# Causal attention into a channel mix on one core: another order on every engine, and a sixth of the operations on another engine

## The chip, the cores and the metric

The kernel runs on one core of a Trainium2 chip. TensorE (PE) multiplies matrices into PSUM, VectorE (DVE), ScalarE (ACT) and GpSimd (POOL) do the elementwise work, SyncE (SP) issues the DMAs. The metric is the device time of one execution in microseconds, the median of three runs.

## The reference

Attention first: four batches of twelve heads, 448 tokens, head dimension 64. Its output, with the heads side by side as 768 features, goes into a channel mix with a hidden width of 1024.

```
scores = q @ k.T / 8;  future tokens masked;  attn = softmax(scores);  x = attn @ v
x_prev = x shifted down by one token, first row 0
xk = mu_k*x + (1-mu_k)*x_prev;   xr = mu_r*x + (1-mu_r)*x_prev
k  = relu(xk @ w_k);   v = (k*k) @ w_v;   r = sigmoid(xr @ w_r)
out = r * v
```

## The kernel before

Two heads make a *pair*; there are 24 pairs, six to a batch, each giving one tile xt of 128 features by 448 tokens. The score rows of a pair are split into chunks of 112 tokens. For each pair TensorE makes the scores (L405, L418), VectorE takes the row maxima (L435), ScalarE or VectorE scales them (L447, L449), ScalarE takes the exponentials (L458). In batch 0 TensorE then transposes the exponentials (L663) and a copy brings them to SBUF (L674); later the probabilities are split into two f16 parts (L639, L643) and transposed by DMA. The product with v (L705) and an evacuation (L722) give xt; the inverse row sums reach xt by way of two small matmuls and a copy (L616, L620, L626, L636).

Once a pair's xt is there, two weighted copies are mixed: a scaling (L249 on ScalarE, L251 on VectorE, L255 on GpSimd, all through the helper `scaled`) and a multiply-add on VectorE (L749), and in later batches a split into f16 parts (L756, L760). A batch's projections run over its six pairs: mk (1024 wide, from xk and w_k) and mr (768 wide, from xr and w_r). In batch 0 they are fp32 matmuls (L981), in later batches three f16 matmuls to a step (L966). k is clipped and squared (L989 or L991, L1005 or L1007), scaled by a common factor that is brought through TensorE (`across`, L270 and L281) and split into f16 parts: the high part by `scaled`, the low part by one instruction on VectorE (L1053) or two on GpSimd (L255 and L1056). Its product with w_v is mv; the last multiplication (L1076) reads mv and r, which was copied out of PSUM (L1061). The accumulators share few PSUM banks, so a new one waits for the instruction that empties an older one.

The weights come in by DMA through three staging buffers: the raw words are taken apart (L840, L848 or L850, L854), the largest element of each half row is found (`w_half`, L806, whose main output `junk` is thrown away), scales are made (L814 to L822) and the f16 parts written (L249, L251 or L255, and L884 or L887). Loads of q and k of a pair have three buffers.

What sets the order: every operation is recorded in a `Plan` (L39) and issued by `Plan.run` in the order of a number each, from the row `starts` in `CHOICE`. Some 722 operations can go to more than one engine, and a letter each in `engines` (A, D, P) says to which. `fills` says where idle matmuls stand (`idle`, L298): pieces of two matmuls of 64 columns, whose results nobody reads. An engine runs its instructions in the order of issue and waits for whatever an instruction needs.

## Time and profile before

| | us |
|---|---|
| median of three runs | 484.56 (483.99 to 485.06) |
| the profiled execution | 485.16 |
| its span in the trace | 483.2 |
| busy in the span: TensorE, VectorE, ScalarE, GpSimd | 466.2, 371.5, 290.3, 202.9 |

The span runs from the first instruction to the last; 1.96 us of the profiled execution lie outside it. A busy share is a mean over stages that differ: the first 60 us are attention of batch 0 with the weights' preparation beside it, later stages are mostly matrix products. TensorE's busy time holds the fillers too.

### The profile page before, as it was taken

The page shows a single profiled execution, that of the slowest core. Times are in us where ns is not written, and L with a number is a line of the kernel's source. Part 1 is how long each engine was busy: PE and PEld are TensorE (multiplying, and loading weights), DVE is VectorE, ACT ScalarE, POOL GpSimd, SP SyncE. Part 2 cuts the span into 40 slices and gives each one's busy share as a digit, 9 for nine tenths or more (in the row PEclk, how much of TensorE's full clock was granted, in tenths as well). Part 3 has the DMA queues.
Part 4 walks back from the last instruction along what each step waited for, and adds up shares of the span by engine and source line. Part 5 has one row for each costly group of instructions (what it writes and reads, how often), then busy time and mean ns, then how long its engine had stood idle before and what let it go on. Part 6 is the DMA issues. An engine that isn't in the chain of part 4 may idle for free.

```text
span 483.2 us, 9633 instructions
## 1 busy us (share of the span) xinstructions
PE 466.2 (96%) x3685; PEld 271.3 (56%) x3685; DVE 371.5 (77%) x724; ACT 290.3 (60%) x814; POOL 202.9 (42%) x174
## 2 busy tenths in 40 slices
PE   8898899999999899999999899999999999999996
PEld 6566665455546566655555556655566565555553
DVE  5999899998898899998788998834879986337021
ACT  5999998996526976678959632645647710110500
POOL 4341461216732263747735723671557665003000
PEclk9999999999999999999999999999999999999999
DMA  8997466881107689391158587353155771000011
GB/s 319 298 333 255 152 213 208 201 217 39 39 1 155 139 191 199 109 165 38 40 102 167 142 177 131 89 112 78 39 96 98 169 146 39 0 1 0 1 57 58
DMA packets 94846, 60.60 MB, mean 125 GB/s; under 512 B 83408, under 2 KB 86480, under 8 KB 94032
## 3 DMA queue, kind: packets, MB, share of 16 engines
q1 hardware_dynamic: 94800, 59.98, 49.7%
q8 instruction: 29, 0.48, 0.4%
q14 instruction: 17, 0.14, 0.1%
HBM read 33.82 MB, written 5.51 MB: 81 GB/s over the span
## 4 chain that ended last, share of the span: by engine, by line
PE 70%; DVE 10%; ACT 9%; DMA 7%; issue 2%; POOL 1%; DVEq 0%; POOLq 0%; ACTq 0%; SPq 0%
PE mk L966 17%; PE mv L966 17%; PE mr L966 9%; PE s L418 7%; PE mk L981 6%; PE bank L705 5%; DMA pT<-p 5%; PE mr L981 4%; ACT e L458 4%; PE s L405 2%; DVE s L435 2%; DMA wraw<-in_w_r_dram 1%; ACT junk L806 1%; DVE pT L674 1%; ACT wk L840 1%
## 5 line engine op out<-in xcount | busy, mean ns | idle before, releaser
L966 PE MATMUL mv<-k,wv 128*128 128x448 f16 x576 | 113.8, 353 | 1.7 <-DVE a L1076 1.7
L458 ACT ACTIVATE e<-s,st 112x224 f32<-112x224 f32 (+3 forms) x192 | 93.3, 497 | 10.2 <-DVE st L449 4.5
L966 PE MATMUL mk<-xk,wk 128*128 128x448 f16 x432 | 83.6, 353 | 0.0
L966 PEld LDWEIGHTS <-wv 128*128 128x128 f16 x576 | 54.5, 98 | 50.9 <-issue 2.5
L435 DVE TENSOR_REDUCE s<-s 112x2 f32<-112x224 f32 (+3 forms) x96 | 70.2, 742 | 13.0 <-PE s L418 11.8
L966 PEld LDWEIGHTS <-wk 128*128 128x128 f16 x486 | 46.5, 98 | 44.6 <-issue 2.2
L966 PE MATMUL mr<-xr,wr 128*128 128x448 f16 x270 | 56.3, 353 | 0.0
L643 DVE TENSOR_TENSOR p<-e,p 112x1120 f16<-112x1120 f32 x27 | 37.4, 1389 | 7.1 <-ACT p L639 3.7
L1076 DVE SCALAR_TENSOR_TENSOR a<-mv,kap,a 128x448 f32<-128x448 f32 x24 | 16.1, 674 | 34.7 <-PE mv L966 34.6
L458 ACT ACTIVATION_READ_ACCUMULATOR e<-s,st 112x1 f32 x192 | 40.1, 209 | 0.0
L981 PE MATMUL mk<-xk,wk 128*128 128x448 f32 x96 | 38.2, 546 | 0.3 <-DVE xk L749 0.3
L966 PEld LDWEIGHTS <-wr 128*128 128x128 f16 x270 | 25.4, 98 | 22.4 <-issue 0.3
L1061 ACT COPY a<-mr 128x448 f32<-128x448 f32 x16 | 8.5, 534 | 37.9 <-PE mr L966 17.7
L749 DVE SCALAR_TENSOR_TENSOR xf<-xt,shares,xf 128x448 f32<-128x448 f32 x36 | 29.8, 841 | 1.0 <-POOL xf L255 0.8
L705 PEld LDWEIGHTS <-vs 112*64 112x64 f16 x648 | 26.9, 110 | 6.1 <-issue 5.1
L705 PE MATMUL bank<-pT,vs 112*64 112x224 f16 (+1 forms) x648 | 29.7, 245 | 0.5 <-DMA pT<-p 0.5
L981 PE MATMUL mr<-xr,wr 128*128 128x448 f32 x72 | 29.2, 547 | 0.0
L850 POOL TENSOR_SCALAR wraw<-wraw 128x768 int32<-128x768 uint16 (+1 forms) x13 | 16.3, 1257 | 25.8 <-DVE pT L674 10.7
L981 PEld LDWEIGHTS mk<-xk,wk 128*128 128x128 f32 x96 | 17.5, 190 | 16.3 <-issue 15.4
L369 POOL TENSOR_TENSOR ql<-qk,qh 128x896 fp32r<-128x896 f32 x8 | 21.0, 2630 | 12.6 <-issue 7.3
L418 PE MATMUL s<-ql,qh 64*112 64x112 f32 (+3 forms) x144 | 25.7, 352 | 0.4 <-POOL ql L369 0.4
L989 ACT ACTIVATE a<-mk 128x448 f32<-128x448 f32 x24 | 13.1, 547 | 21.1 <-PE mk L966 20.5
(219 smaller groups left out, 909.5 us busy)
## 6 DMA issues: line engine op xcount, KB each, us to landing
qk<-in_qk_dram SPq DMA_DIRECT2D x24, 448.0 KB, 3.7
wraw<-in_w_k_dram SPq DMA_DIRECT2D x6, 1024.0 KB, 10.3
wraw<-in_w_v_dram SPq DMA_DIRECT2D x8, 768.0 KB, 4.6
vraw<-in_v_dram SPq DMA_DIRECT2D x24, 224.0 KB, 3.0
out_dram<-a SPq DMA_DIRECT2D x24, 224.0 KB, 2.1
wraw<-in_w_r_dram SPq DMA_DIRECT2D x6, 768.0 KB, 4.7
pT<-p SPq DMA_TRANSPOSE x36, 4.9
muT<-in_mu_dram SPq DMA_DIRECT2D x1, 6.0 KB, 13.2
```

Source lines behind the costliest of these rows:

```text
L369: tt[e](t, qkt.pop(w), qkh[w].bitcast(F32), ALU.subtract)
L418: nc.tensor.matmul(s[:CP, j, o : o + n], q_[rows, 0, c * CP : (c + 1) * CP], k_[rows, 1, :n], start=False, stop=c == max(STEPS[g]) and i = ...
L435: nc.vector.tensor_reduce(stat[w][:, c, :] if flipped(w) else most(w, g, c, c + 1), s[:CP, :, o : o + CP * (c + 1)], AX.X, ALU.max, negate ...
L458: nc.scalar.activation(em[w, j][:, blocks(c)].rearrange("p a b -> p (a b)"), sps[w, g][:CP, j, o : o + CP * (c + 1)], AF.Exp, bias=stat[w] ...
L643: tt[e](p[:, NB:, :CP], em.pop((w, j)), p[:, :NB, :CP], ALU.subtract)
L705: nc.tensor.matmul(px[w][64 * j : 64 * j + 64, cols], value(j, vi), p(j, pi), start=n == 0 and i == 0, stop=last and i == len(steps) - 1, ...
L749: nc.vector.scalar_tensor_tensor(f, x_of(w)[:, :S], share(w, mu, 1), f, ALU.mult, ALU.add)
L850: nc.gpsimd.tensor_scalar(t, u, TOP3, -0.499, ALU.mult, ALU.add)
L966: nc.tensor.matmul(ps, w[:, wi, cols], x[:, xi, t0 : t0 + n], start=(i == 0 and a == 0), stop=(i == steps - 1 and a == 2),)
L981: nc.tensor.matmul(mps[m, kind, o][:, :n], z[:, o * P : (o + 1) * P], x, start=i == 0, stop=i == NO - 1)
L989: nc.scalar.activation(a, mps[m, "k", f][:, :n], AF.Relu)
L1076: nc.vector.scalar_tensor_tensor(s, mps.pop((m, "v", o))[:, : M[m][2]], kap[m][:, 3:4], s, ALU.mult, ALU.mult)
```

## The change

Only three rows of `CHOICE` differ: the numbers in `starts` (2161 of them), 353 of the 722 letters of `engines` (of A, D and P there were 260, 322 and 140, now 253, 318 and 151), and `fills` (24 entries as before, but 103 pieces in place of 153, so 206 filler matmuls in place of 306, of which 20 now stand behind the start of the dense part). The list of operations is the same; a few operations take two instructions on one engine and one on another.

```
-    "fills": [[1300,14],[6745,15],[11149,16],[15068,5],[19523,3],[23646,1],...
+    "fills": [[4358,14],[9432,10],[12788,10],[16261,1],[20040,2],[25465,6],...
```

Three places, as the instructions stand on their engine. Names carry a pair's number (e_2_1 is the second head's exponentials of pair 2) or a batch and block (k2_3_5); the last number only tells tiles apart.

ScalarE at the exponentials of pair 2, up to its last one, before:

```order
L458 ACTIVATE e_2_1_491,su_2_490<-s_2_0_429,st_2_465 112x112
L806 ACTIVATE junk_91,wn_149<-wk_144 128x512
L674 COPY pT_1_0_474<-eT_1_0_2_498 112x448
L674 COPY pT_1_1_527<-eT_1_1_0_505 112x336
L447 ACTIVATE st_2_465<-s_2_1_483 112x2
L806 ACTIVATE junk_91,wn_149<-wk_144 128x512
L458 ACTIVATE e_2_0_496,su_2_490<-s_2_1_483,st_2_465 112x336
L458 ACTIVATE e_2_1_491,su_2_490<-s_2_1_483,st_2_465 112x336
L447 ACTIVATE st_2_465<-s_2_2_515 112x2
L674 COPY pT_1_1_527<-eT_1_1_2_545 112x448
L458 ACTIVATE e_2_0_496,su_2_490<-s_2_2_515,st_2_465 112x448
L458 ACTIVATE e_2_1_491,su_2_490<-s_2_2_515,st_2_465 112x448
```

and now, from the second exponential of pair 2 to the first of pair 3:

```order
L458 ACTIVATE e_2_1_405,su_2_398<-s_2_0_385,st_2_394 112x224
L458 ACTIVATE e_2_0_399,su_2_398<-s_2_0_385,st_2_394 112x112
L458 ACTIVATE e_2_1_405,su_2_398<-s_2_0_385,st_2_394 112x112
L458 ACTIVATE e_2_0_399,su_2_398<-s_2_1_415,st_2_394 112x336
L458 ACTIVATE e_2_1_405,su_2_398<-s_2_1_415,st_2_394 112x336
L840 ACTIVATE wk_144<-wraw_3_351 128x1024
L806 ACTIVATE junk_91,wn_149<-wk_144 128x512
L636 COPY xt0_92<-sp_0_462 128x448
L458 ACTIVATE e_2_1_405,su_2_398<-s_2_2_443,st_2_394 112x448
L458 ACTIVATE e_2_0_399,su_2_398<-s_2_2_443,st_2_394 112x448
L674 COPY pT_1_1_469<-eT_1_1_1_501 112x336
L458 ACTIVATE e_3_0_520,su_3_519<-s_3_0_473,st_3_515 112x112
```

Of the half-row pieces (L806) fewer stand among the exponentials: 21 stood ahead of pair 5's last one, now 10 do. Copies of L636 have come here from VectorE.

VectorE ahead of the mix of pair 5's xk (`xk_5`), before:

```order
L369 TENSOR_TENSOR ql_7_1347<-qk_7_1196,qh_7_1341 128x896
L822 RECIPROCAL wm_146<-wm_146 128x1
L722 TENSOR_TENSOR xt1_93<-bank_142,xt1_93 128x448
L435 TENSOR_REDUCE s_6_2_1316<-s_6_2_1316 112x2
L884 SCALAR_TENSOR_TENSOR wv_1138<-wz_13_1265,wm_146,wv_1138 128x768
L251 TENSOR_SCALAR xk_5_1384<-xt1_93,sharesp_154 128x448
L854 SCALAR_TENSOR_TENSOR wz_14_1349<-wz_14_1349,wraw_14_1290 128x768
L749 SCALAR_TENSOR_TENSOR xk_5_1384<-xt1_93,sharesp_154,xk_5_1384 128x448
```

and now:

```order
L722 TENSOR_TENSOR xt1_93<-bank_142,xt1_93 128x448
L435 TENSOR_REDUCE s_7_0_1190<-s_7_0_1190 112x2 x2
L449 TENSOR_SCALAR st_7_1225<-s_7_0_1190 112x4
L816 TENSOR_SCALAR wm_146<-wm_146 128x1
L884 SCALAR_TENSOR_TENSOR wv_969<-wz_12_1063,wm_146,wv_969 128x768
L818 TENSOR_SCALAR wm_146<-wm_146 128x1
L749 SCALAR_TENSOR_TENSOR xk_4_1207<-xt0_92,sharesp_154,xk_4_1207 128x448
L822 RECIPROCAL wm_146<-wm_146 128x1
L749 SCALAR_TENSOR_TENSOR xk_5_1212<-xt1_93,sharesp_154,xk_5_1212 128x448
```

The evacuation (L722) and the mix stand 20 and 17 rows earlier in the list; the last L369, L854 and L251 ahead of the mix are behind it or on other engines, and a reduction for pair 7 stands ahead of it.

GpSimd's last rows, batch 3, before:

```order
L756 CAST xk_23_5384<-xf0_23_5366 128x448
L760 TENSOR_TENSOR xk_23_5384<-xf0_23_5366,xk_23_5384 128x448
L760 TENSOR_TENSOR xr_21_5399<-xf1_21_5379,xr_21_5399 128x448
L255 TENSOR_TENSOR xf1_22_5415<-xt2_94,shares_152 128x448
L255 TENSOR_TENSOR a_156<-a_156,tf_3_5617 128x448
L1056 TENSOR_TENSOR k2_3_5_5669<-a_156,k2_3_5_5669 128x448
```

and now:

```order
L760 TENSOR_TENSOR xr_20_5300<-xf1_20_5294,xr_20_5300 128x448
L255 TENSOR_TENSOR xf1_21_5303<-xt1_93,shares_152 128x448
L760 TENSOR_TENSOR xr_21_5325<-xf1_21_5303,xr_21_5325 128x448
L255 TENSOR_TENSOR xf1_22_5328<-xt2_94,shares_152 128x448
L255 TENSOR_TENSOR a_156<-a_156,tf_3_5519 128x448
L1056 TENSOR_TENSOR k2_3_1_5526<-a_156,k2_3_1_5526 128x448
```

There k2_3_5 is block 5 of k in batch 3. Before, GpSimd made the low part of one block; now of six: behind the pair shown for block 1, five more such pairs follow, for blocks 4, 3, 6, 7 and 5.

SyncE's loads stand in another order too: qk of pair 5 behind the third load of w_r.

## Rows read from the trace of the kernel before

**Rows 1.** The profile page, parts 1 and 2: busy us (share) xinstructions; granted clock

```profile
PE 466.2 (96%) x3685; PEld 271.3 (56%) x3685; DVE 371.5 (77%) x724; ACT 290.3 (60%) x814; POOL 202.9 (42%) x174
...
PEclk9999999999999999999999999999999999999999
```

**Rows 2.** Busy us by stretch (x instructions), then PEclk, DMA share, GB/s

```profile
0.00:60.00 60.00, 52.24 (x669) 36.87 (x669) 52.13 (x113) 52.22 (x165) 22.12 (x37) 1.00 0.82 273
60.00:82.40 22.40, 21.63 (x182) 13.19 (x180) 21.46 (x42) 21.66 (x66) 9.67 (x9) 1.00 0.61 214
82.40:165.20 82.80, 81.78 (x414) 43.53 (x415) 73.64 (x164) 58.31 (x156) 31.68 (x23) 1.00 0.49 115
...
380.00:483.20 103.20, 99.55 (x618) 53.26 (x615) 44.66 (x90) 16.51 (x35) 22.80 (x18) 1.00 0.21 49
```

**Rows 3.** Fillers, by line: busy us, mean ns, then idle before

```profile
L298 PE MATMUL bank<-busy 128*128 128x64 f16 x306 | 14.3, 202 | 0.2 <-DVE xt L722 0.2
```

**Rows 4.** TensorE's timeline at 82 and at 166 us: start, length, idle before, releaser

```profile
82.43 2.52 PE L981 MATMUL mk<-xk,wk 128*128 128x448 f32 x6 [0.28 <-DVE xk L749]
...
165.96 0.73 PE L966 MATMUL mv<-k,wv 128*128 128x448 f16 x3 [1.69 <-DVE a L1076]
```

**Rows 5.** VectorE's timeline ahead of 82.43

```profile
80.84 1.53 DVE L749 SCALAR_TENSOR_TENSOR xk<-xt,sharesp,xk 128x448 f32<-128x448 f32 x1
```

**Rows 6.** Busy us between 20 and 40 us

```profile
20.00:40.00 20.00, 18.06 (x247) 13.02 (x246) 18.91 (x40) 19.97 (x67) 6.63 (x8) 1.00 0.95 320
```

**Rows 7.** VectorE's timeline at 39 us

```profile
39.48 0.67 DVE L325 TENSOR_REDUCE vm<-vraw 112x1 f32<-112x512 f32 x1
40.07 1.21 DVE L854 SCALAR_TENSOR_TENSOR wk<-wk,wraw 128x1024 uint32<-128x1024 uint32 x1
```

**Rows 8.** Single lines: count, ns min/median/max, first and last start us, form

```profile
L636 DVE COPY xt<-sp x12: 604/614/626, 19.2 to 391.7; 128x448 f32<-128x448 f32 x12
...
L636 ACT COPY xt<-sp x12: 510/534/621, 52.9 to 394.5; 128x448 f32<-128x448 f32 x12
...
L251 DVE TENSOR_SCALAR xk<-xt,sharesp x4: 443/679/1093, 35.9 to 79.6; 128x448 f32<-128x448 f32 x4
...
L369 DVE TENSOR_TENSOR ql<-qk,qh x10: 1074/1080/1275, 75.9 to 303.0; 128x896 fp32r<-128x896 f32 x10
...
L884 DVE SCALAR_TENSOR_TENSOR wv<-wz,wm,wv x6: 966/1004/1007, 74.3 to 105.2; 128x768 f16<-128x768 f32 x6
...
L854 DVE SCALAR_TENSOR_TENSOR wz<-wz,wraw x8: 942/949/959, 68.6 to 109.8; 128x768 uint32<-128x768 uint32 x8
...
L848 ACT ACTIVATE wraw<-wraw x7: 884/912/981, 47.1 to 108.4; 128x768 int32<-128x768 uint16 x7
```

**Rows 9.** ScalarE's timeline at 16 and at 59 us

```profile
16.11 0.66 ACT L806 ACTIVATE junk<-wk 128x512 f16<-128x512 f32 x1
...
16.73 0.56 ACT L458 ACTIVATE e<-s,st 112x336 f32<-112x336 f32 x1
...
59.12 0.46 ACT L458 ACTIVATE e<-s,st 112x224 f32<-112x224 f32 x1
```

**Rows 10.** The page's part 6: loads, KB each, median us from issue to landing

```profile
qk<-in_qk_dram SPq DMA_DIRECT2D x24, 448.0 KB, 3.7
```

**Rows 11.** K's scaling on GpSimd, copy of r on ScalarE, by line

```profile
L255 POOL TENSOR_TENSOR a<-a,tf x4: 932/2036/3156, 135.2 to 441.5; 128x448 f32<-128x448 f32 x4
...
L1061 ACT COPY a<-mr x16: 520/532/568, 130.8 to 453.0; 128x448 f32<-128x448 f32 x16
```

**Rows 12.** GpSimd's timeline at 249 and at 441 us

```profile
249.09 0.93 POOL L255 TENSOR_TENSOR a<-a,tf 128x448 f32<-128x448 f32 x1
...
441.49 3.16 POOL L255 TENSOR_TENSOR a<-a,tf 128x448 f32<-128x448 f32 x1 [34.23 <-DVE k L251]
444.73 1.03 POOL L1056 TENSOR_TENSOR k<-a,k 128x448 f16<-128x448 f32 x1
```

**Rows 13.** VectorE's timeline at 442 us

```profile
441.99 1.87 DVE L1053 SCALAR_TENSOR_TENSOR k<-a,tf,k 128x448 f16<-128x448 f32 x3
```

More of the change, by code (lines that the diff above doesn't have):

```diff
@@ L95 @@
-    "engines": "PPPPPPADADADAPADDDDDDDPPAAADDDDDDAADADADADPPADDDDAADDDDDADDADAADDDPDDDPPADDDAADDDPPDDADDDADDPAAPPPAPDDPDDPADPADADDADDADDAAPADPAAAAAAAAAAAADDAAADADADADPDADPDAPPPDDPDPDPDADADDDPDADDDADDAAADDPPDDADADPPADPDPDAPAPPDPDADDDAADPDDAADAAADDPDAAPDADADDDAPPDAADADAPDAPDADDADDDDDDDAAADADDAPDDDPDPAPPAPAAADDADDAPDPDAAPAADADAADADAPAAAPAPAPPDAPDDPPADDDADPADAADAAADDAAAAAAADAAAADADADADADAPADADAAAAAAAAADAAADDDAPDAADPDDDAAADADDAPDADAPDAAADADAADDDDPDPDAPPDDDDADAPAAADADDAPPAPAPDAAAPAPADADADPDPAADPDADDADDPADPDPDDPPDPDDDDDDDDDDDPDDPAPAADDADADAAADAAAADDADADPDADADADDPADDADDADDDDAADAADADADAPDAPDDAPAPADDAPDDPDADPDDPDAPPPPAPPAPPDPADAAPADADADPDAPDDPDAPADADDAPAAAPDPPDDPDPDPAADPDPPDDADAPAAPPADPPDDAADDDDDPPDDDDDDDADADADAADDDDDDDDDDDDDDDPDDDDADAAAA",
@@ new lines @@
+    "engines": "PPPPPPDAADDAPPDADDADDDPPDDDPPAADDDDADPDDADAPDADDDAADPDDDAPDADAAADAADDDPPADADDDAAAPPDADDDADDAPPPPPAPDAPPDDADDADDPDDPADADDPPDAADADAAADADDAAAAAAAAPADADADADADPDDDPDADDDPDADPDPDADPDDDPDADADAAAAADDDDDPDAPDDADDDDDADPPDDAAAAAAPPDADPPDADADPPDDPDADADDDADDDDAAADPPDDPDPDDADAAPDDADAADAPDAAPADDPPAADAPAAAADDDADDDADDDPDDPPDDADADADDAPDPPDPPPAPPDAPAAADADDDDDAPAAAAADAADAAAAADDADAPAPAPADADDDDDADAAAAAAAAADADAAAPDAADDDPDAAADADDADDPPADAADPDPDDDDDDDAPDAAPADAAADDPPAAADDDDDDDDDADAADPDADDAPDDPAAPDDPADADDADPPDAPPAPAPPADPDDDDADADAPDDDAAPDAADDDAAAADAADDDPDDDADADPPAPADADAADDDAAAAAADPPDDDDDDADDDPPDAAPPDDPPADDAPDADPPPDADPPPPDPPDDDPDAAAADPPAADDADPPPPDPAPDDDPDADDDPDADAAPPDPDDAADADDPADPDAPAPPPDDDDDPAAADADDADADDDAAAAADDDDAADADADDAPADAPAPAPAPDPDADADA",
@@ L97 @@
+    "fills": [[4358,14],[9432,10],[12788,10],[16261,1],[20040,2],[25465,6],[29602,3],[32890,1],[32891,7],[33260,1],[34435,1],[34620,3],[34945,2],[39897,3],[43831,15],[44886,2],[45393,1],[46161,3],[54848,6],[61621,2],[125763,2],[134158,4],[179277,1],[180230,3]],
 }
```

3 lines of the change are left out of this document (1 added, 2 removed).

## The prediction

> **What bounds the kernel now.** I read the page's first two parts first: TensorE is busy 96% of the span and its granted clock stands in the top digit in every slice [rows 1]. So time can only come out of TensorE's idle time, out of its filler matmuls, or out of its real work, and the real work is the same before and after. Next I read the busy times by stretch [rows 2]. TensorE is idle 7.8 us of the first 60 (60 - 52.24), 0.8 of the next 22.4, 1.0 of the 82.8 after that, 3.7 of the last 103.2. The 306 fillers take 14.3 us, all before 63.4 us [rows 3]. So some 23 us without useful work (7.8 + 0.8 + 14.3) lie ahead of 82.4 us, and far less lies behind. What ends that start is seen in TensorE's own timeline and VectorE's: the first matmul of the batch-0 projection that reads the mixed tile of pair 5 starts at 82.43, released by VectorE's mix (L749), which began at 80.84 and lasted 1.53 [rows 4, 5]. From there TensorE runs nearly without a gap; the only long one is 1.69 us at 165.96, ahead of mv_0_2, whose accumulator waits for VectorE's multiplication (L1076) [rows 4]. In the first 60 us both VectorE (52.13) and ScalarE (52.22) are full, between 20 and 40 us ScalarE 19.97 of 20 and VectorE 18.91 [rows 2, 6]. So the start is bound by the list of things that these two engines do ahead of pair 5's mix, and it gets shorter by what is taken out of that list.
>
> **The change part by part.**
> *VectorE's list up to the mix of xk_5.* An instruction there costs its duration less about 0.08 us, because the next starts before its end: the reduction at 39.48 lasts 0.67 but the next starts at 40.07, 0.59 later [rows 7]. Four copies of L636 go to ScalarE or behind: 4 x (0.614 - 0.08) = 2.1. Four L251 on xk at 0.679 - 0.08 = 0.60 become one of the shortest kind, 0.443 - 0.08: 2.0. Three reductions L325: 3 x 0.59 = 1.8. One L369: 1.0. One L884 on wv: 0.9. One L854 on wz: 0.9 [rows 7, 8]. That is 8.7. Some dozen small instructions that go besides (2.3 us by the medians of their lines, an estimate) and eight that come (two reductions L435, a mix, four small ones: 2.4 us, likewise) cancel. So the list is 8.7 us shorter.
> *ScalarE's list up to pair 5's last exponential.* Eleven of 21 pieces of L806 (largest element of a half weight row) go behind: one piece with its accumulator read takes 0.62 us, 16.11 to 16.73, so 11 x 0.61 = 6.7 [rows 9]. One L848 goes to GpSimd (0.9), three L636 come (3 x 0.53 = 1.6), and small ones give 1.5 net by their medians [rows 8]: 7.5 in all. These pieces are only put off; the weights that need them are read by the f16 products of batch 1 and later, and other ScalarE work of that later time hides them, as ScalarE is busy 58.31 of 82.8 there [rows 2]; without that cover the 6.7 would come back.
> VectorE and ScalarE feed each other, so pair 5's mix moves by between 7.5 and 8.7; I take 8.2. TensorE has 0.8 us less real work ahead of it (59.5 to 58.7, summed along both lists), so 7.4 of it is gain. TensorE itself is no bound: its work ahead of that point was about 82.4 - 7.8 - 0.8 - 14.3 = 59.5, is now 58.7, and 186 of the 206 fillers stand there, 186 x 47 ns = 8.7 (14.3 / 306 = 47 ns [rows 3]); 67.4 is below 82.4 - 8.2 = 74.2.
> *Loads.* SyncE issues qk of pair 5 now behind the third load of w_r, which waits for a free staging buffer, so it leaves at about 38 us (an estimate from the sums of the lists), and a qk load takes 3.7 us to land in the median [rows 10]. ScalarE began pair 5's exponentials at 59.12 [rows 9], now some 7.5 earlier, near 51.6; the cover is about 10 us, less the split and the score products. If it were gone, the start would slip by what is missing.
> *From xk_5 to mv_0_2.* VectorE was idle 82.8 - 73.64 = 9.2 us there [rows 2]. Its list up to the multiplication that mv_0_2 waits for grows by 7.3 us (six L884, mostly at 0.7 to 0.9, 4.8; two squares 1.1; two L636 1.1; one L369 1.0; a second L1076 0.6; against them mainly a reduction, a copy of r and parts of v, which go), in time 7.3 x 73.64 / 71.0 (its list as summed from medians) = 7.6. TensorE gets 3.8 us more real work in between (36 products with V, four score blocks, eight spreads, one step) and 12 fillers, 0.6. If all of VectorE's idle time stays, TensorE waits 1.69 + 7.6 - 4.4 = 4.9 there, 3.2 more than before; if the new work fills idle time, the 1.69 goes. Between +3.2 and -1.7 I take the middle, +0.7.
> *Late fillers.* Twenty stand behind 82 us now, where before had none: 0.9 at most, 0 where TensorE waits anyhow; 0.6.
> *Behind 165 us* VectorE's list to each later release is shorter or equal, and TensorE's idle time is small already. GpSimd gets eleven operations more, some 9 us on 202.9 [rows 1]. The nearest price of a new wait is the 1.69 of [rows 4], below it nothing: 0.8, rounded to 0.7 because the last batch is priced as a rival.
> Sum on the profiled run, which took 485.16 (span 483.2 and 1.96 around it): 485.16 - 7.4 + 0.7 + 0.6 + 0.7 = 479.8. That run lies 0.6 above the median 484.56 of the runs shown, so 479.2.
>
> **A place where the move speaks against the change.** In the last batch GpSimd takes the low part of six of the eight k blocks (a scaling L255, then a subtraction L1056); before it took one. The scaling lasts 0.93 to 3.16 us, median 2.04: 0.93 at 249.09, but 3.16 from 441.49, while VectorE ran L1053, which reads two tiles, from 441.99 [rows 11 to 13]. The subtraction took 1.03 at 444.73.
> The Trainium skill, GPSIMD Engine Reference, section 8 (Key points), says that GpSimd shares its SBUF interfaces with VectorE and contends with VectorE instructions in a two-port mode or with two SBUF inputs, and that VectorE is structurally about twice as fast at elementwise work. The trace agrees: the same form takes 3.4 times as long beside L1053 as at 249.09. By that rule the six pairs would cost some 4.2 us each if VectorE were as busy there as before, and 2.0 each if not, as priced next.
>
> **Rivals.**
> *Slower: the chain on GpSimd before mv_3_1.* mv_3_1 needs the PSUM buffer that a copy of r (L1061, 0.53 on ScalarE [rows 11]) frees, and that copy's slot is the one of the last of the six blocks. From the scale's broadcast to mv_3_1 TensorE has 19.1 us of work. The chain is 1.1 (rest of the scale, seven small VectorE instructions) + 0.7 (the first scaling to f16, L249 on ScalarE; both estimates) + 6 N + 0.5. With N = 0.93 + 1.03 = 1.96 it is 14.1, nothing shows; with the median, 2.04 + 1.03 = 3.07, it is 20.7, a stall of 1.6; with 3.16 + 1.03 = 4.19 it is 27.4, a stall of 8.3: 479.2 + 8.3 = 487.5. The gain of 5.4 is gone from N = 3.7 on. For it: 3.16 was measured at this place. Against it: VectorE has seven long instructions there now (two L251, two L1053, three L1061), where before it had sixteen (eight, seven, one), so N should stay near 2 to 3.
> *No change: the start is bound by the weights' arrival.* The DMA engines' share was 0.95 between 20 and 40 us, 0.82 over the first 60 [rows 2, 6], and loads of weights and q, k are re-ordered. Then the mix stays near 82, the shorter lists only wait, and the time is 484 to 485. Against it: ScalarE was 19.97 of 20 busy there, so it did not wait.
> *Later: VectorE keeps all its idle time up to 165 us.* +3.2 in place of +0.7: 481.7, up to 483.5 if the mix also moves by only 7.5 and the late fillers show.
> *Faster still: all of 7.9 (8.7 - 0.8) is kept, the wait of 1.69 goes, and nothing is late.* 485.16 - 7.9 - 1.7 + 0.6 - 0.6 = 475.6.
>
> **How the numbers follow.** The forecast, 479.2 with 477.3 to 481.3 around it, gets 0.52; faster still 0.15; later 0.11; no change 0.08; slower by the GpSimd chain 0.14. A difference of about 0.2%, 1 us, is what a measurement of this kernel can tell from none. So faster 0.78, same 0.08, slower 0.14. The range reaches from the lowest case, 475.3, to 485.5: it takes in no change and the smaller stalls, and leaves out the larger stalls (0.1) and little below.
>
> **What would show it.** The first matmul on xk_5 near 74 in place of 82.43, with VectorE's mix still its releaser, shows the start right; at 80 or later, the loads' rival. TensorE's wait ahead of mv_0_2 tells the middle: 0 to 5 us. Fillers should be 206 and their time 9.7. In the last batch the L255 and L1056 rows on GpSimd give N, and a gap ahead of mv_3_1 the stall. Span minus TensorE's busy time, with the fillers added, should shrink from 31.3 (483.2 - 466.2 + 14.3) by some 5 us. The forecast is wrong if ScalarE's put-off pieces show as waits for weight preparation behind 90 us.

## The result and the profile after

The changed kernel takes 479.86 us (median of 8 runs, 478.46 to 486.59; the highest is left out of the ratio), the kernel before 484.60 in the same runs: a ratio of 0.9906, interval 0.9878 to 0.9934. Run again later it had 479.74 and 0.9878 (0.9842 to 0.9914). So it is about 1% faster, some 5 us, and the forecast of 479.2 with its range holds it.

The profiled execution of the changed kernel took 480.65, its span is 478.9. The page's first parts (busy time and share; the granted clock in 40 slices), then the same stretches as in [rows 2] (the last ends at the new span's end):

```profile
PE 463.1 (97%) x3585; PEld 268.7 (56%) x3585; DVE 362.9 (76%) x718; ACT 294.1 (61%) x815; POOL 186.9 (39%) x186
...
PEclk9998999999999999999999999999999999999999
```

```profile
0.00:60.00 60.00, 52.81 (x588) 36.13 (x590) 51.39 (x106) 50.55 (x158) 28.24 (x46) 0.97 0.81 279
60.00:82.40 22.40, 22.39 (x158) 13.52 (x159) 21.43 (x43) 21.03 (x58) 8.05 (x9) 1.00 0.51 162
82.40:165.20 82.80, 82.12 (x486) 45.26 (x486) 74.20 (x177) 65.88 (x175) 26.93 (x23) 1.00 0.50 119
...
380.00:478.90 98.90, 94.69 (x590) 50.48 (x587) 36.75 (x70) 23.63 (x48) 25.52 (x25) 1.00 0.22 52
```

The reader is to see two things. TensorE's busy time fell by 3.1 (466.2 to 463.1 [rows 1]), about what the fillers lost (14.3 to 11.3, below; 9.7 was forecast), and its idle time by 1.2. And the clock, which was in the top digit throughout, has one digit of 8 now: 0.97 over the first 60 us. Span less busy time, with the fillers added, went from 31.3 to 27.1, 4.2 where some 5 were forecast.

Fillers by line, then TensorE's timeline where the first matmul on xk_5 and mv_0_2 now lie, and VectorE's timeline at pair 5's mix, for [rows 3 to 5]:

```profile
L298 PE MATMUL bank<-busy 128*128 128x64 f16 x206 | 11.3, 206 | 0.9 <-DVE xt L722 0.9
```

```profile
74.70 3.55 PE L981 MATMUL mk<-xk,wk 128*128 128x448 f32 x9
...
162.62 0.37 PE L626 MATMUL sp<-rt,sel 128*128 128x112 f16 x4
162.82 1.49 PE L966 MATMUL mv<-k,wv 128*128 128x448 f16 x7
```

```profile
74.07 0.68 DVE L749 SCALAR_TENSOR_TENSOR xk<-xt,sharesp,xk 128x448 f32<-128x448 f32 x1
...
74.74 0.67 DVE L749 SCALAR_TENSOR_TENSOR xk<-xt,sharesp,xk 128x448 f32<-128x448 f32 x1
```

The mix ends at 74.74 + 0.67 = 75.4, in place of 82.4. TensorE does not wait for it: the first matmul on xk_5 is the fifth record of the nine in the row at 74.70 and starts at 76.20, and no bracket stands there, as TensorE is busy 22.39 of 22.40 in that stretch. At 162.82, ahead of mv_0_2, the wait of 1.69 is gone. In a second profile of the changed kernel, from the later run (experiment 9), the mix stands here and ends at 74.4:

```profile
73.73 0.67 DVE L749 SCALAR_TENSOR_TENSOR xk<-xt,sharesp,xk 128x448 f32<-128x448 f32 x1
```

Because the orders differ, the same clock time does not mean the same progress. The table compares when each kernel has done a given amount of real work on TensorE, fillers left out (each matmul counted with the mean that its kind has in the trace before; an estimate of the place, while the times are from the traces). The second profile had its clock at 0.999.

| real work done, us | before | changed | earlier by | second profile | earlier by |
|---|---|---|---|---|---|
| 25 | 40.98 | 37.70 | 3.3 | 37.49 | 3.5 |
| 40 | 61.86 | 56.37 | 5.5 | 55.37 | 6.5 |
| 59.4 (xk_5 before) | 82.43 | 76.96 | 5.5 | 75.95 | 6.5 |
| 160 | 185.24 | 179.34 | 5.9 | 178.58 | 6.7 |
| 180 | 205.46 | 200.79 | 4.7 | 200.05 | 5.4 |
| 449 (end) | 478.44 | 474.10 | 4.3 | 473.01 | 5.4 |

So all of the gain is made ahead of 60 us, the middle keeps it, and about 1.2 to 1.6 us are lost behind.

Where the clock fell in the profiled execution (stretches of 1 us; columns as above), and the same stretches of the second profile:

```profile
32.00:33.00 1.00, 0.56 (x5) 0.44 (x5) 1.00 (x3) 1.00 (x4) 1.00 (x1) 1.00 0.58 203
...
34.00:35.00 1.00, 0.13 (x3) 0.04 (x2) 1.00 (x3) 0.90 (x4) 0.92 (x3) 1.00 0.75 246
35.00:36.00 1.00, 1.00 (x14) 0.96 (x14) 1.00 (x1) 0.08 (x1) 0.92 (x2) 0.60 1.00 412
...
37.00:38.00 1.00, 1.00 (x10) 1.00 (x12) 0.55 (x1) 1.00 (x2) 0.92 (x2) 0.50 0.34 43
```

```profile
33.00:34.00 1.00, 0.70 (x7) 0.44 (x5) 1.00 (x3) 1.00 (x4) 1.00 (x1) 1.00 0.46 152
...
35.00:36.00 1.00, 0.13 (x5) 0.09 (x4) 1.00 (x3) 0.99 (x4) 0.92 (x3) 1.00 0.89 307
36.00:37.00 1.00, 1.00 (x18) 0.92 (x17) 1.00 (x1) 0.41 (x2) 0.92 (x2) 1.00 0.94 393
```

In the first, TensorE is busy 0.13 of the microsecond ahead of the fall, then runs at the lower of its two levels (1.2 in place of 2.4 GHz) for 3.4 us, half of which, 1.7, is lost. In the second, the same hole of 0.13 is there and the clock stays. At 40 us of work the first is 1.0 behind the second. At 10 us of work it was 1.2 ahead (17.54 against 18.75 us), because the second had a slow start of its own (last section); so it lost 2.2 in between.

The scaling on GpSimd by line, GpSimd's timeline at the end of the last batch, and ScalarE's last copy of r there, for [rows 11, 12]:

```profile
L255 POOL TENSOR_TENSOR a<-a,tf x12: 932/1008/2015, 120.0 to 442.8; 128x448 f32<-128x448 f32 x12
```

```profile
432.00 0.93 POOL L255 TENSOR_TENSOR a<-a,tf 128x448 f32<-128x448 f32 x1 [21.78 <-ACT k L249]
433.01 1.29 POOL L1056 TENSOR_TENSOR k<-a,k 128x448 f16<-128x448 f32 x1
...
442.80 0.93 POOL L255 TENSOR_TENSOR a<-a,tf 128x448 f32<-128x448 f32 x1
443.81 1.04 POOL L1056 TENSOR_TENSOR k<-a,k 128x448 f16<-128x448 f32 x1
```

```profile
448.06 0.53 ACT L1061 COPY a<-mr 128x448 f32<-128x448 f32 x1 [6.28 <-PE mr L966]
```

Six blocks take from 432.00 to 444.85, so N is 2.14. The copy at 448.06 was released by TensorE's mr, not by GpSimd; the chain ends 3 us ahead of the need. mv_3_1 starts at 449.51, inside a row of 23 matmuls without a wait.

Pair 5's load and exponentials, for [rows 9, 10] (SyncE's and ScalarE's timelines):

```profile
37.80 0.43 SPq L355 DMA_DIRECT2D qk<-in_qk_dram  x1
```

```profile
51.78 0.45 ACT L458 ACTIVATE e<-s,st 112x224 f32<-112x224 f32 x1
```

The load leaves at 37.80 (forecast 38), the exponentials begin at 51.78 (forecast 51.6).

### The profile page after: what moved, and what is told of

It reads as the page before. It is cut to its first block, busy times and chain, and to the rows that moved or that the text cites. A ratio compares the mean times of both kernels' runs of the same rounds, so it can differ in the third digit from the quotient of the medians.

```text
span 478.9 us, 9469 instructions
## 1 busy us (share of the span) xinstructions
PE 463.1 (97%) x3585; PEld 268.7 (56%) x3585; DVE 362.9 (76%) x718; ACT 294.1 (61%) x815; POOL 186.9 (39%) x186
## 4 chain that ended last, share of the span: by engine, by line
PE 75%; DVE 10%; DMA 8%; ACT 5%; issue 2%; POOL 1%; DVEq 0%; ACTq 0%
PE mv L966 18%; PE mk L966 17%; PE mr L966 8%; PE mk L981 8%; PE s L418 7%; DMA pT<-p 6%; PE bank L705 6%; PE mr L981 4%; ACT e L458 3%; DVE s L435 2%; PE s L405 2%; PE eT L663 1%; DMA wraw<-in_w_r_dram 1%; ACT p L639 1%; DVE p L643 1%
## 5 line engine op out<-in xcount | busy, mean ns | idle before, releaser
L458 ACT ACTIVATE e<-s,st 112x336 f32<-112x336 f32 (+3 forms) x192 | 93.0, 492 | 28.8 <-DVE st L449 17.3
L435 DVE TENSOR_REDUCE s<-s 112x2 f32<-112x224 f32 (+2 forms) x96 | 70.8, 743 | 17.6 <-PE s L418 12.1
L643 DVE TENSOR_TENSOR p<-e,p 112x1120 f16<-112x1120 f32 x26 | 35.5, 1374 | 5.1 <-ACT p L639 4.2
L458 ACT ACTIVATION_READ_ACCUMULATOR e<-s,st 112x1 f32 x192 | 38.6, 201 | 0.0
L749 DVE SCALAR_TENSOR_TENSOR xf<-xt,shares,xf 128x448 f32<-128x448 f32 x36 | 27.1, 752 | 10.0 <-ACT xf L249 6.0
L639 POOL CAST p<-e 112x1120 f16<-112x1120 f32 x12 | 14.7, 1228 | 48.0 <-ACT e L458 21.9
L643 POOL TENSOR_TENSOR p<-e,p 112x1120 f16<-112x1120 f32 x10 | 24.1, 2412 | 11.7 <-ACT p L639 11.6
L639 ACT CAST p<-e 112x1120 f16<-112x1120 f32 x18 | 20.1, 1124 | 10.2 <-DMA pT<-p 10.1
L405 PEld LDWEIGHTS <-pick 64*112 64x112 bf16 x288 | 15.3, 127 | 19.1 <-issue 15.7
```

Of the source, the lines that this page charges most:

```text
L405: nc.tensor.matmul(diagonal, pick[rows, h], fill, start=h == 0, stop=False, skip_group_check=True)
L435: nc.vector.tensor_reduce(stat[w][:, c, :] if flipped(w) else most(w, g, c, c + 1), s[:CP, :, o : o + CP * (c + 1)], AX.X, ALU.max, negate ...
L458: nc.scalar.activation(em[w, j][:, blocks(c)].rearrange("p a b -> p (a b)"), sps[w, g][:CP, j, o : o + CP * (c + 1)], AF.Exp, bias=stat[w] ...
L639: copy[e](p_t[at_][:, :NB, :CP], em[w, j])
L643: tt[e](p[:, NB:, :CP], em.pop((w, j)), p[:, :NB, :CP], ALU.subtract)
L749: nc.vector.scalar_tensor_tensor(f, x_of(w)[:, :S], share(w, mu, 1), f, ALU.mult, ALU.add)
```

## The experiments

Each timed against the kernel before on the same chip; ratios with 95% intervals. The changed kernel's is 0.9906 (0.9878 to 0.9934).

### 1. The order without the engines

```
-    "engines": "PPPPPPDAADDAPPDADDADDDPP...   (changed)
+    "engines": "PPPPPPADADADAPADDDDDDDPP...   (before)
```

> The changed order and fillers with the engines of before. Up to the mix of xk_5, VectorE's list is then 1.8 us shorter than before and ScalarE's 6.8 (sums of medians along the lists; with both changes they are some 7 to 8.7 and 7.7). Theory (the longer of the two lists sets the start, so order and engines are worth something only together): the mix of xk_5 ends near 80.5 in place of 82.4, and the time is about 483 (481.5 to 485), perhaps more where the order does not suit the engines later on. Rival 1 (what ScalarE puts off is the gain, VectorE follows): mix near 76, time 479 to 481. Rival 2 (the gain is only the 100 fillers left out): 480.

620.56 us, ratio 1.2717 (1.2650 to 1.2783). What TensorE waited for most (us in all, times, longest), and the clock:

```profile
PE s L405 <- ACT e L458: 26.0, 17, 4.5
```

```profile
PEclk9998989895999899898897978989989898989999
```

All of the expectations missed, by 27%. Sums of lists up to one mix say nothing here. The waits (26 us for exponentials, all through the program) suggest that an instruction stands at a place that fits one engine, and on the other holds up what follows; the clock, 0.936 in this profile, comes on top. Order and engine letters are one choice.

### 2. The engines without the order

```
-    "engines": "PPPPPPADADADAPADDDDDDDPP...   (before; its order and fillers stay)
+    "engines": "PPPPPPDAADDAPPDADDADDDPP...   (changed)
```

> The order and the fillers of before with the new engines. VectorE's list up to the mix of xk_5 is 6.3 us shorter than before, ScalarE's 2.4 longer, GpSimd's 5.5 longer. Theory (the longer list sets the start): no gain, mix at 82 to 85, time 484.5 to 488. Rival 1 (VectorE's list alone sets it): mix near 76 to 77, time 479 to 481. Rival 2 (only fillers count): 484.5, as before, since the fillers are those of before.

518.16 us, 1.0672 (1.0637 to 1.0708); clock 0.972 in the profile. The theory had the sign and not the size, it seems for the same reason as in 1. These two runs do not tell which list sets the start; 6 and 7 do.

### 3. The old fillers in the changed kernel

```
-    "fills": [[4358,14],[9432,10],[12788,10],...
+    "fills": [[1300,14],[6745,15],[11149,16],...
```

> The changed kernel with the 306 fillers of before at their old times in the schedule. In the changed kernel the clock fell to half for 3.4 us at 35.2 us, behind a stretch of 3 us in which TensorE was busy for only half of the time. Theory (fillers fill waits that VectorE and ScalarE set, and keep the clock up): the 100 fillers more, 4.4 us, lie partly in waits; 480 to 482, and the clock stays at 1.00. Rival (TensorE's own list sets the start of the changed kernel, so each filler is paid): 479.9 + 4.4 - 1.7 (the clock's loss that goes) = 482.6 or more.

482.79 us, 0.9943 (0.9919 to 0.9967): 2.9 above the changed kernel's 479.86, as the rival had it; by the ratios 1.8, and the intervals overlap. VectorE's timeline in its profile (clock 1.000):

```profile
77.89 0.66 DVE L749 SCALAR_TENSOR_TENSOR xk<-xt,sharesp,xk 128x448 f32<-128x448 f32 x1
```

The mix is 3.1 later than at 74.74, and 4.2 later than at 73.73 in the second profile, where the clock did not fall either. So of the 4.4 us of 100 more fillers, at places that were made for another order, most are paid at the mix, and in the time some 2 to 3. Whether their number or their places cost this is not told apart.

### 4. The new fillers in the kernel before

```
-    "fills": [[1300,14],[6745,15],[11149,16],...
+    "fills": [[4358,14],[9432,10],[12788,10],...
```

> The kernel before with only the new row of fillers, 206 in place of 306. Theory (in the kernel before VectorE and ScalarE set the start, fillers lie in the waits): no gain, 484.5 within 1, or slower by 1 to 4 where the clock falls to half in the start. Rival (the gain of the change is the fillers left out): 480 to 481.

495.09 us, 1.0186 (1.0141 to 1.0230): slower by 9 by the ratio, more than the 1 to 4 expected. The stretch from 40 to 60 us, and TensorE's timeline at its beginning:

```profile
40.00:60.00 20.00, 15.90 (x132) 9.55 (x132) 15.12 (x33) 14.21 (x40) 1.72 (x2) 0.68 0.48 158
```

```profile
41.64 1.41 PE L663 MATMUL eT<-ident,e 112*112 112x112 f32 x6 [2.35 <-DVE pT L674]
```

With the wait of 2.35 the clock fell; over the 20 us it is 0.68. TensorE at the lower level is late for the others too: VectorE and ScalarE are busy 15.12 and 14.21 of 20, where they were busy 18.67 and 18.85 in the kernel before. So the new row of fillers does not carry the gain by itself: with the old order it costs 9 us. The old order with some of its own fillers left out was not run.

### 5. More fillers where the clock fell

```
-    [33260,1],[34435,1],
+    [33260,8],[34435,8],
```

> The changed kernel with 14 more pieces of fillers (28 matmuls, 1.2 us by 44 ns from start to start) at two places between 32.7 and 34.4 us, where TensorE stood idle before its clock fell to half at 35.2. Theory (the clock falls behind idle time, and the new fillers lie in waits that VectorE sets): granted clock 1.00 in the profile and in most runs, the spread of the runs (478.5 to 486.6 in the changed kernel) shrinks, median 478.5 to 479.5. Rival (fillers are paid in full, the clock falls elsewhere): 480 to 481 with the same spread.

479.31 us, 0.9861 (0.9835 to 0.9887); mean clocks 0.999 to 1.000 in all six runs, 478.49 to 480.97. As the theory had it, yet the interval overlaps the changed kernel's two, and experiment 9's second kernel, with the same 14 pieces, had runs at 0.993 and 0.996. That these fillers hold the clock is not shown.

### 6. ScalarE's put-off pieces back

```
     "starts": (22 of the 24 numbers of w_half)
-    17308, 36442, 67601, 66373, ...
+    15589, 17039, 18403, 18403, ...
```

> The changed kernel with the pieces of L806 back at the places that they had in the kernel before (behind as many exponentials as there): 21 in place of 10 ahead of pair 5's last exponential, 6.7 us more on ScalarE, nothing else moved. Theory (ScalarE's list sets the start as much as VectorE's): pair 5's mix at 80 to 82 in place of 75.4, time 484 to 486. Rival (VectorE's list alone sets it, ScalarE has room): mix at 75 to 77, 479.5 to 481.

493.61 us, 1.0149 (1.0109 to 1.0188). Its stretch from 60 to 82.4 us, pair 5's mix on VectorE, and TensorE's longest wait ahead of it:

```profile
60.00:82.40 22.40, 19.26 (x128) 11.97 (x126) 13.65 (x28) 17.08 (x52) 8.79 (x8) 0.70 0.43 144
```

```profile
87.59 0.67 DVE L749 SCALAR_TENSOR_TENSOR xk<-xt,sharesp,xk 128x448 f32<-128x448 f32 x1
```

```profile
64.20 0.21 PE L616 MATMUL rp<-identh,rs 112*128 112x112 f16 x1 [3.06 <-ACT xt L636]
```

Pair 5's last exponential on ScalarE, here and in the changed kernel:

```profile
67.11 0.67 ACT L458 ACTIVATE e<-s,st 112x448 f32<-112x448 f32 x1
59.71 0.63 ACT L458 ACTIVATE e<-s,st 112x448 f32<-112x448 f32 x1
```

That exponential is 7.4 later for 6.7 us of ScalarE's work: ScalarE's list does set the start. The mix ends at 88.3, 12.9 later, and VectorE, busy 13.65 of 22.40, waits. The rest of the price is that TensorE waited (3.06 for a copy that now stands behind those pieces) and then ran at 0.70 of its clock over 22.4 us, up to 6.7 lost.

### 7. Eight operations back on VectorE

```
     "engines": (spread_out of pairs 0, 1, 2, 5; scaling of xk of pairs 1, 2, 4, 5)
-    A, A, A, A; P, P, A, A
+    D, D, D, D; D, D, D, D
```

> The changed kernel with four copies (L636, pairs 0, 1, 2, 5) and four scalings of xk (L251, pairs 1, 2, 4, 5) back on VectorE as in the kernel before, order and all else as changed: 4 x 0.53 + 4 x 0.60 = 4.5 us more on VectorE ahead of pair 5's mix, some 3.2 less on ScalarE, 1.2 less on GpSimd. Theory (VectorE's list sets the start): mix at 79 to 80 in place of 75.4, time 483 to 484.5. Rival (ScalarE's list or TensorE's own work sets it): mix within 1 us of 75.4, 479 to 480.5.

485.14 us, 0.9990 (0.9968 to 1.0012); clock 1.000 in the profile. Pair 5's mix:

```profile
78.47 0.67 DVE L749 SCALAR_TENSOR_TENSOR xk<-xt,sharesp,xk 128x448 f32<-128x448 f32 x1
```

It ends at 79.1, 3.7 later than at 75.4, and 4.7 later than in the second profile of the changed kernel (74.4), whose clock did not fall there either, for 4.5 us of VectorE's work. The theory holds: VectorE's list sets the start too. The time went a little above the expected 483 to 484.5, and all of the gain is gone.

### 8. GpSimd's chain made long

```
             scaled(a, a, r, e)
-            tt[e](t[:, 1], a, t[:, 0], ALU.subtract)
+            for _ in range(3 if b == 3 else 1):
+                tt[e](t[:, 1], a, t[:, 0], ALU.subtract)
```

> The changed kernel with the subtraction L1056 on GpSimd done three times over in batch 3 (same values): each of the six blocks costs 2.14 + 2 x 1.03 = 4.2 us there in place of 2.14 (12.85 us for six in the changed kernel's trace, from 432.00). Theory (mv_3_1 waits for the copy of r that the last block sets free): GpSimd ends at 432.0 + 25.2 = 457.2, mv_3_1 starts near 458 in place of 449.5, time 487 to 488.5. Rival (mv_3_1 does not hang on GpSimd's last block): 480 within 1.

491.67 us, 1.0103 (1.0079 to 1.0127). GpSimd's last rows, TensorE at mv_3_1, and TensorE's next 3.2 us:

```profile
454.29 0.93 POOL L255 TENSOR_TENSOR a<-a,tf 128x448 f32<-128x448 f32 x1
455.31 3.25 POOL L1057 TENSOR_TENSOR k<-a,k 128x448 f16<-128x448 f32 x3
```

```profile
459.17 3.15 PE L966 MATMUL mv<-k,wv 128*128 128x448 f16 x8 [7.41 <-ACT a L1062]
```

```profile
459.20:462.40 3.20, 3.20 (x9) 1.25 (x9) 0.00 (x0) 3.19 (x5) 0.00 (x0) 0.50 0.00 0
```

mv_3_1 starts at 459.17, 9.7 later than at 449.51 (458 expected), behind a wait of 7.41 for the copy of r (L1061, a line lower in this kernel). So the rival's mechanism is real, and its wait was put at 8.3 for N = 4.2: with it the gain is more than gone. The time is 3 above the expectation. Some 1.6 of it is the clock, which fell in the wait and stood at 0.50 for the 3.2 us behind it; 1.2 is that mv_3_1 starts later than the 458 expected.

### 9. The changed kernel again, without late fillers, without any, and with the low parts back

Four kernels on one chip. The changed kernel itself:

> The changed kernel itself, unaltered, beside the three that follow, so that they can be compared on one chip. 479.9 within 1, with some runs above 482 at a mean clock of 0.99 to 0.996.

479.74 us, 0.9878 (0.9842 to 0.9914), as expected.

With the 14 pieces of experiment 5 and without the 20 late fillers:

```
-    ,[125763,2],[134158,4],[179277,1],[180230,3]],
+    ],
```

> The kernel with 14 more pieces of fillers at 32.7 to 34.4 us, and without the 20 fillers that stand behind 82 us. Theory (late fillers lie on TensorE's own path, 20 x 44 ns = 0.9 us, and the clock does not need them): 478.4 to 479, 0.5 to 0.9 below the kernel with the 14 pieces alone (479.3). Rival (they lie in waits or keep the clock up): the same, or slower by 1.7 in the runs in which the clock falls for 3.4 us.

481.59 us, 0.9895 (0.9854 to 0.9936), runs from 478.33 to 483.74: no gain that could be told. Four of its six runs had a mean clock of 0.999 or 1.000 and still lie between 478.33 and 482.12, so the clock's fall is not the reason; what is, is not known.

Without fillers:

```
-    "fills": [[4358,14],[9432,10],...
+    "fills": [],
```

> The changed kernel without any filler, 206 matmuls less. Theory (fillers keep the granted clock up in the start, and lie mostly in waits): the clock falls to half for 15 us or more ahead of 60 us, 3.4 us at a time, each costing half its length; 487 to 500. Rival (fillers are only a load): 479.9 - 9.1 = 471 to 475.

480.30 us, 0.9879 (0.9841 to 0.9916). The theory fell and the rival too: 206 matmuls less made no difference that could be told. Three stretches of its profile and pair 5's mix:

```profile
20.00:40.00 20.00, 17.52 (x163) 10.51 (x163) 19.52 (x42) 19.45 (x62) 10.78 (x12) 1.00 0.78 253
40.00:60.00 20.00, 17.33 (x157) 11.54 (x152) 18.49 (x36) 18.82 (x58) 9.27 (x11) 0.91 0.85 279
...
0.00:75.89 75.89, 64.34 (x542) 40.76 (x543) 66.12 (x139) 66.31 (x202) 34.91 (x52) 0.98 0.77 263
```

```profile
74.42 0.67 DVE L749 SCALAR_TENSOR_TENSOR xk<-xt,sharesp,xk 128x448 f32<-128x448 f32 x1
```

The mix ends at 75.1, as with fillers (75.4 and 74.4), TensorE's first matmul on xk_5 starts at 75.9 (76.2 and 75.2), and VectorE and ScalarE are about as full between 20 and 40 us (19.52 and 19.45 of 20) as [rows 6] had them. Up to that matmul TensorE is idle some 11.5 us (75.89 less 64.34); with fillers it was 7.2 and 5.8. The fillers' time has become waiting, so in these profiles they lie in waits that the other two engines set. The clock did fall, 0.91 between 40 and 60, but not by the 15 us of the theory. All six runs had a mean clock of 0.985 to 0.996, against 0.996 to 1.000 with fillers on this chip. Whether fillers cost about what they save of the clock, so that the two cancel in the median, is not told apart.

The low parts of blocks 1, 3, 4, 6, 7 of batch 3 on VectorE:

```
     "engines": (low parts of batch 3, blocks 1, 3, 4, 6, 7)
-    P, P, P, P, P
+    D, D, D, D, D
```

> The changed kernel with the low parts of k blocks 1, 3, 4, 6 and 7 of batch 3 back on VectorE (L1053, 0.67 us each) as in the kernel before; block 5 stays on GpSimd. Theory (GpSimd's chain, 12.85 us for six, ends ahead of TensorE's need in the changed kernel, so it neither cost nor gave anything): 479.9 within 0.8. Rival (the move to GpSimd was part of the gain, as VectorE's copies of r come sooner): 481 to 483.

481.50 us, 0.9903 (0.9870 to 0.9935). It is 1.8 above the changed kernel's median here, and the intervals overlap widely; neither expectation is borne out, and the profile (span 478.3 against 477.8) shows 0.5. What the move to GpSimd gave is under what these runs can tell.

## Why the prediction was right, step by step

*The start.* Forecast: mix 8.2 earlier (7.5 to 8.7), of it 7.4 gain. Measured: 7.0 in the profile whose clock fell, 8.0 in the second; gain at equal work 5.5 and 6.5. The mechanism was right: both lists are shown binding (6, 7). The step that failed is "TensorE itself is no bound". The first matmul on xk_5 was to start at 74.2, released by VectorE's mix; it starts 0.8 behind the mix's end, at 76.20 and in the second profile at 75.20, without a wait. The sum 67.4 counted work and fillers and left out the idle time that TensorE has ahead of that point anyhow. TensorE up to 76.20, in all and its fillers alone:

```profile
0.00:76.20 76.20, 69.00 (x727) 46.43 (x728) 66.62 (x139) 66.06 (x201) 35.10 (x52) 0.98 0.76 262
...
0.00:76.20 76.20, 10.11 (x186) 8.59 (x186) 0.98 0.76 262
```

So it is 58.9 of work with the clock's fall in it (58.7 in the sum), 10.1 of fillers (8.7) and 7.2 of idle time (nothing: the sum took 7.8 and 0.8 of idle time off the kernel before and put none back). That idle time is not TensorE's own making: without any filler the matmul came no sooner (75.9 in experiment 9). The lists hold TensorE up earlier, at the exponentials and their transposes, not at the mix, as the first two of these waits of the changed kernel show (us in all, times, longest; the third belongs to *Behind*):

```profile
PE eT L663 <- ACT e L458: 2.1, 3, 1.2
...
PE eT L663 <- DVE pT L674: 1.0, 2, 0.8
...
PE rp L616 <- POOL rs L610: 0.9, 1, 0.9
```

How large the gain of the start is, these profiles tell only to some 2 us: the first has the clock's fall in it and the second the slow start. The profiles of experiment 5 and of experiment 9's second kernel have neither, but 28 fillers more in the start. There the mix ends at 72.9 and 72.6, earlier than the range had it, and the work that stood at 82.43 before is reached 8.0 and 8.3 earlier (the estimate of the table). Experiment 5's mix:

```profile
72.23 0.67 DVE L749 SCALAR_TENSOR_TENSOR xk<-xt,sharesp,xk 128x448 f32<-128x448 f32 x1
```

So the forecast of 7.4 lies among the measured values, 5.5 to 8.3, and is not shown to be too large or too small.

*Ahead of mv_0_2.* Forecast +0.7, between +3.2 and -1.7. The wait is gone; up to 160 us of work the gain grew by 0.2 to 0.4. VectorE's 7.6 us more was mis-sized. From the first matmul on xk_5 to mv_0_2, before and now:

```profile
82.43:165.96 83.53, 81.78 (x414) 43.53 (x415) 74.37 (x166) 59.04 (x158) 31.68 (x23) 1.00 0.49 114
76.20:162.90 86.70, 86.02 (x491) 47.28 (x490) 78.17 (x182) 69.73 (x183) 28.12 (x24) 1.00 0.47 116
```

VectorE is busy 3.8 us more there and TensorE 4.2, so the wait went although VectorE's idle time hardly shrank (9.2 to 8.5). The true value lay in the lower part of the bounds.

*Behind.* Forecast 0.6 for late fillers and 0.7 for GpSimd's new work, which was put at some 9 us more on that engine; its busy time fell by 16.0 (202.9 to 186.9), so that reading was wrong in sign. Measured 1.6 and 1.2 from 160 us of work on; most of it between 160 and 180, where TensorE's wait of 0.9 for row sums on GpSimd (the third of the waits shown above, at 184.14) lies and eight of the late fillers stand. That leaving those fillers out gains anything is not shown (9). The put-off pieces of ScalarE show no wait for weight preparation behind 90 us: TensorE's largest there is 1.9 in all, for exponentials.

*The sum* of 5.4 came out as 4.3 and 5.4. In the second profile that is partly luck: by its numbers the start's 0.9 too much and the middle's 0.9 too little cancel. The range's low end, 475.3, is not the lowest case as it was worked out, which is 475.6.

*The rivals.* GpSimd's chain: N was 2.14, in the range of 2 to 3 that was expected, and the prediction's reason, that VectorE has little to do there, agrees with the trace; the rival is real at N = 4.2 (8). The scaling's median fell from 2036 ns [rows 11] to 1008. By the Trainium skill, GPSIMD Engine Reference, section 8 (Key points), GpSimd and VectorE contend for shared SBUF interfaces. The trace agrees: the three scalings of the last batch with no VectorE instruction beside them took 0.93 or 0.94, against 3.16 [rows 12]. But GpSimd is not always the one that waits, as the price of 4.2 us a pair took it to be. Beside the scaling of 432.00, which took 0.93, VectorE ran this L1053, 1.37 where the median of that line is 0.68:

```profile
432.04 1.37 DVE L1053 SCALAR_TENSOR_TENSOR k<-a,tf,k 128x448 f16<-128x448 f32 x1
```

The loads' rival is out: the mix moved. The "only fillers" reading, which the busy time suggests at first (3.1 us less, 100 fillers less), is out by the run without any, and 4 does not bear it out.

*What was not priced* is the clock, and how far two runs of one program differ in the start. Identical programs had mean clocks between 0.986 and 1.000; in the runs of the kernel before on the last chip, 0.996 went with 486.9 to 487.4 and 1.000 with 484.7 to 485.6, so one such fall costs some 2 us, twice the 1 us that the prediction put as the resolution.

## What to carry to other kernels

A list of work on one engine that another engine waits for is priced by summing it, but the waiting engine's own idle time belongs into its sum, or it seems to have room that it has not. An order and the assignment to engines that were found together can't be judged, or undone, one without the other: half of this change costs 7 to 27%. Before a filler is called a cost or a help, run without it: beside two full engines leaving 206 of them out could not be told from nothing, while most of 100 more, at other places, was paid. Before two profiles are compared late, compare them early: two of the same program were 1.2 us apart at 18 us.

## What the runs showed of the hardware that had not been expected

TensorE's clock fell in one profile of the changed kernel behind a hole of 0.13 busy in a microsecond, and in the other, with the same hole, it did not. That other profile was slow at its start instead. The same three score matmuls, first profile and second:

```profile
8.71 0.98 PE L418 MATMUL s<-qk 64*112 64x448 f32 x3
8.72 1.81 PE L418 MATMUL s<-qk 64*112 64x448 f32 x3
```

The granted clock reads 1.00 there in both, so this loss, 1.2 us by 10 us of work, does not stand in a run's mean clock. Of the eleven profiles with the changed order six have it (1, 7, 8 and in 9 the first, third and fourth kernel). The Trainium skill, TensorE: Matmul & The Clock Gate, Part 1, says that the number of slow matmuls at a kernel's start varies from run to run; the trace agrees. The runs show such a difference 35 us in as well: there the clock of one program falls in one run and stays in another.

A stall of TensorE is paid twice where the clock falls in it: in experiment 8, 7.41 of waiting, and then 3.2 us at half the clock, 1.6 lost.
